# One condition for the middle and the long arm of an expert block, a branch hint for the next block in both, and 49 narrow idle products at the head in place of 15 wide ones

## The chip, the cores and the metric

The kernel runs on one core of one Trainium2 chip. The metric is device microseconds (us) of one execution, median of several. TensorE (PE) multiplies, with its weight loads shown as an engine of their own (PEld); VectorE (DVE), ScalarE (ACT) and GpSimd (POOL) do the rest; SyncE (SP) issues most transfers.

## The reference

```python
attn_out = sigmoid(q k^T / sqrt(64) - log(448)) v       # 4 x 12 heads, 448 tokens
x = attn_out as 1792 tokens x 768
do_compute = x @ w_skip > 0                              # other tokens pass as they are
e_idx = argmax(xc @ w_gate); gate_w = softmax prob. of that expert
for e in range(8):                                       # 768 -> 1024 -> 768
    y[mask] = gate_w * (relu(xc[mask] @ w1[e]) @ w2[e])
x[do_compute] = xc + y
h = x @ w_in; g = elu(h); out = g @ w_out                # 768 -> 2048 -> 768
```

Everything is float32. The kernel gets that accuracy out of products on split operands: a high and a low part of each side, three products per tile.

## The kernel before

The work runs in three stages: attention (up to about 200 us of the span), the experts (about 200 to 420 us), and the last dense layer pair (to the end). The order on PE, ACT and DVE is written out by hand; only semaphores between engines hold an instruction back.

At the very head `keep_warm` lets PE multiply zeros while the first q and k come in: 15 products, each 512 columns wide, each with its own weight load.

The routing sorts the tokens that compute into blocks of 256 slots, each block for one expert, full blocks first. Block 0 is done ahead of the routing's end (`first_block`). For the others the code is unrolled in `level(i, k)`, i = 1 to 14, each nested in the one before; how many of them run, and which way, is known only on the chip. `k` is the kind of block i, read from `kinds`: 0 no block, 1 at most 128 rows, 2 up to 64 rows in the second half, 3 more than that. With these inputs blocks 1 and 2 are of kind 3, blocks 3 and 4 of kind 2, blocks 5 to 7 of kind 1, and block 8 doesn't exist (the token counts of each expert give it, and the four places of `rest`'s product, in the table below, agree).

In program order, the code of one level is:

- condition `more{i}` (k > 0); else the way out (`close(i)`, far behind, after all levels)
- `between(i)`: 12 flips of the block's rows into columns, and chunks 5 and 6 of the block before (24 products)
- condition `two{i}` (k > 1); else the **short arm**
- `lead_in(i)`: chunk 7 of the block before (12 products)
- condition `few{i}` (k == 2): the **middle arm**, `expert(i, k, (P, FEW))`; else `rest()`
- condition `many{i}` (k == 3): the **long arm**, `expert(i, k, (P, P))`; else `rest()`
- the short arm: `lead_in(i)` and `expert(i, k, (P,), following)`
- then level i + 1

`rest()` is one tiny product, one tiny ACT copy and one tiny DVE copy into a tile of its own. `skips(label, value)` gives PE's sequencer a hint for the condition of that label: 1, it will fall through; 0, it will jump. The hints of before: `two{i}` at the start of a level, `few{i}` ahead of `lead_in`, `many{i}` inside the middle arm, `more{i+1}` inside the short arm.

The weights come in 8 chunks per expert of 128 x 1536, each split by ACT (L547, high part) and DVE (L549, low part) two chunks ahead of PE.

Of the kernel before, what the change touches and what calls it, by code (L numbers as in the profile page):

```python
# [12 lines left out]
F32 = mybir.dt.float32  # L13
# [10 lines left out]
P = 128  # L24
# [14 lines left out]
NB = 1 + (NT + E * (BLK - 1)) // BLK  # L39
# [12 lines left out]
FEW = 64  # L52
# [39 lines left out]
def build(nc, tc, a):  # L92
    q, k, v, consts = a["q"], a["k"], a["v"], a["consts"]
    wg, w1, w2, wi, wo, out = a["wg"], a["w1"], a["w2"], a["wi"], a["wo"], a["out"]
    wide = [w[f].bitcast(I32) for f in range(KF2) for w in (wi, wo)]
    with ExitStack() as top:
# [6 lines left out]
        cst = cp.tile([P, LASTING], F32, name="cst")  # L103
# [10 lines left out]
        iota_h = cp.tile([P, P], F16, name="iota_h")  # L114
# [62 lines left out]
        with ExitStack() as st:  # L177
# [16 lines left out]
            pss = pst.enter_context(tc.tile_pool(name="pss", bufs=3, space=PSUM))  # L194
# [7 lines left out]
            zero_b = xp.tile([P, 1, P], BF16, name="zero_b")  # L202
            nc.gpsimd.memset(zero_b, 0.0)

            def keep_warm(n):

                ps = pss.tile([P, 4, P], F32, name="idle", tag="ps")
                for _ in range(n):
                    nc.tensor.matmul(
                        ps, zero_b[:, 0], zero_b.to_broadcast([P, 4, P]), start=True, stop=True  # L210
                    )

            keep_warm(15)
            xT = xp.tile([P, NP, NT], F32, name="xT")
            lgT = xp.tile([P, RING * P], F32, name="lgT")

# [488 lines left out]
            def tiles(pool, names, shape, dt=F32):  # L705
                return [pool.tile([P, *shape], dt, name=n) for n in names]
# [3 lines left out]
            acc_t = tiles(psb, [f"acc{j}" for j in range(6)], [512])  # L710
# [31 lines left out]
            def routing():  # L742
# [58 lines left out]
                for k_, p in enumerate(counted):  # L801
                    nc.tensor.matmul(
                        ordered, ones_b, p, start=(k_ == 0), stop=(k_ == len(counted) - 1)
# [34 lines left out]
                for t in range(NTT):  # L838
# [17 lines left out]
                tokb = st.enter_context(  # L856
                    tc.tile_pool(name="tokb", reuse_waits="tile", bufs=1, side="right")
                )
                for e in range(2):
                    rest_t.append(iter(tiles(tokb, [f"rest{e}{j}" for j in range(2 * NB)], [1])))  # L860
                hs_t.extend(tiles(tokb, ["hs0", "hs1"], [N1]))
                hf_t.extend(tiles(tokb, ["hf0", "hf1"], [N1]))
                yf_t.extend(hf[:, :N2] for hf in hf_t)
# [9 lines left out]
                yield  # L873
                order_rows()

            rest_t, hs_t, hf_t, yf_t, one_hot = [], [], [], [], []
            last_rows, last_gate, last_slot = [], [], []

            def h_columns(nh, sizes):
# [41 lines left out]
            def ahead(i, c, **parts):  # L921
                c += 2
                split_w(i + c // 8, c % 8, **parts)
# [21 lines left out]
            def up_two(i, soon):  # L945
                for c in range(4):
                    ahead(i, c)
                    for f in range(4):
                        if (c, f) == (0, 1):
                            soon()  # L950
                        up_one(i, c, f)
                        if c % 2:
                            h_one(4 * (c // 2) + f)

            def up_parts(i, sizes, soon):
                for h, n in enumerate(sizes):
                    if n < P:
                        t = h * P
                        nc.scalar.copy(x2[:, 0, :, t + n : t + P], x2[:, 1, :, t : t + n])
                ahead(i, 0)  # L960
                for nh in range(2):
                    for c3 in range(2):
                        c = 2 * nh + c3
                        for h, n in enumerate(sizes):
                            o = acc_t[nh if n == P else (3, 0)[nh]]
                            product(o, h, n, x_part, i, c, N1, 3 * c3, KD)
                        if c == 0:
                            soon()
                        ahead(i, c + 1)
                        if nh == 1 and c3 == 0:  # L970
                            h_columns(0, sizes)
                    for n in sizes:
                        if n == P:
                            nc.scalar.copy(hs_t[nh], acc_t[nh])
                        else:
                            nc.scalar.copy(hf_t[nh], acc_t[(3, 0)[nh]])

            def back(i, h, n, chunks):

                for c in chunks:  # L980
                    c4, nh = divmod(c - 4, 2)
                    product(py[nh][h], h, n, h_part, i, c, N2, 4 * c4, KF1)
                    if n < P and c4:
                        nc.scalar.copy(yf_t[nh], py[nh][h])
# [23 lines left out]
                slot_order()  # L1008
                return kind(1)

            def expert(i, k, sizes, following=None):
                whole = sizes == (P, P)

                def soon():
                    outcome(i - 1, 0, P)

                if whole:
                    up_two(i, soon)
                    ahead(i, 4)
                else:  # L1020
                    up_parts(i, sizes, soon)
                    if len(sizes) > 1:
                        skips(f"many{i}", 1 - (k >> 1))
                    elif i + 1 < NB:
                        skips(f"more{i + 1}", (following + 3) >> 2)
                ahead(i, 5)
                for h, n in list(enumerate(sizes))[1:]:
                    if whole:
                        back(i, h, n, range(4, 8))
                        outcome(i, h, n)  # L1030
                        back(i, 0, P, range(4, 5))
                    else:
                        back(i, h, n, range(4, 6))
                        h_columns(1, sizes)
                        back(i, h, n, range(6, 8))
                        back(i, 0, P, range(4, 5))
                        outcome(i, h, n)
                if len(sizes) == 1:
                    back(i, 0, P, range(4, 5))
                    h_columns(1, sizes)  # L1040

            def outcome(i, h, n):
                gated(xg_t[i % NXG][h], slot_gate[:, 2 * i + h : 2 * i + h + 1], h, n)
# [32 lines left out]
            def pass_on(i):  # L1076

                gather(i + 1)
                if i > 1:
                    scatter(i - 2)
# [86 lines left out]
            def close(i):  # L1172
                if i == 1:
                    gather(1)
                s = 2 * (i - 1)
                nc.gpsimd.tensor_copy(last_rows[0], xg_t[(i - 1) % NXG][0])
                nc.gpsimd.tensor_copy(last_gate[0], slot_gate[:, s : s + 1])
                nc.gpsimd.tensor_copy(last_slot[0], slot_tok[:, s : s + 1])
                give(xg_t[(i - 1) % NXG][1], slot_tok[:, s + 1 : s + 2])
                for g in range(3):  # L1180
                    flip_rows(i, g, ends[g])
                for g in range(3):
                    flip_rows(i + 1, g, later[g])
# [21 lines left out]
            def kind(i):  # L1205
                return nc.values_load(kinds[:1, i : i + 1], min_val=0, max_val=3)

            def skips(label, unless=0):

                tc.mark_branch_hint_location(label, hint=unless, engines=[ET.PE])  # L1210

            def rest():

                nc.tensor.matmul(acc_t[5][:, :2], iota_h, iota_h[:, :2], start=True, stop=True)
                nc.scalar.copy(next(rest_t[0]), cst[:, :1])
                nc.vector.tensor_copy(next(rest_t[1]), cst[:, :1])

            def level(i, k):
                pass_on(i)
                if i == NB:  # L1220
                    close(i)
                    return
                with tc.If(k > 0, label=f"more{i}") as more:
                    skips(f"two{i}", k >> 1)
                    fetch(i, range(2, 8))
                    between(i)
                    fetch(i + 1, range(2))
                    following = kind(i + 1) if i + 1 < NB else 0
                    with tc.If(k > 1, label=f"two{i}") as both:
                        skips(f"few{i}", 1 - (k & 1))  # L1230
                        lead_in(i)
                        with tc.If(k == 2, label=f"few{i}") as arm:
                            expert(i, k, (P, FEW))
                        with arm.Else():
                            rest()
                        with tc.If(k == 3, label=f"many{i}") as arm:
                            expert(i, k, (P, P))
                        with arm.Else():
                            rest()
                    with both.Else():  # L1240
                        lead_in(i)
                        expert(i, k, (P,), following)
                    level(i + 1, following)
                with more.Else():
                    close(i)
# [229 lines left out]
```

## Time and profile before

| | |
|---|---|
| median of 3 runs | 904.13 us (903.27 to 906.42) |
| the profiled execution | 903.78 us, of which the span from first to last instruction is 902.0 us |
| PE, its busy share | 880.9 us, 98% |
| PEld | 710.4 us, 79% |
| DVE, ACT, POOL | 62%, 54%, 9% |
| `rest`'s product (L1214) | 4 times: at 214.1, 249.3, 310.2 and 346.5 us |

A row of the timeline reads: start, duration, engine, line, operation, output <- inputs, shapes, count, and in brackets how long the engine sat idle before it and what ended that; "issue" there means that it waited for nothing that the profile shows. "q8 instruction" among the DMA queues is code on its way to an engine.

### The profile page before, as it was taken

The page shows a single profiled execution, that of the slowest core. Times are in us where ns is not written, and L with a number is a line of the kernel's source. Part 1 is how long each engine was busy: PE and PEld are TensorE (multiplying, and loading weights), DVE is VectorE, ACT ScalarE, POOL GpSimd, SP SyncE. Part 2 cuts the span into 40 slices and gives each one's busy share as a digit, 9 for nine tenths or more (in the row PEclk, how much of TensorE's full clock was granted, in tenths as well). Part 3 has the DMA queues.
Part 4 walks back from the last instruction along what each step waited for, and adds up shares of the span by engine and source line. Part 5 has one row for each costly group of instructions (what it writes and reads, how often), then busy time and mean ns, then how long its engine had stood idle before and what let it go on. Part 6 is the DMA issues. An engine that isn't in the chain of part 4 may idle for free.

```text
span 902.0 us, 13626 instructions
## 1 busy us (share of the span) xinstructions
PE 880.9 (98%) x5208; PEld 710.4 (79%) x5208; DVE 557.5 (62%) x872; ACT 485.5 (54%) x680; POOL 80.8 (9%) x79
## 2 busy tenths in 40 slices
PE   9999999999999898998999999999999999999998
PEld 4445545699999787887888888888888888888997
DVE  2968778697666465885888886444344444344664
ACT  7777776554455464773645554434444434344664
POOL 1000000112101022332100000100000100000100
PEclk9999999999999999999999999999999999999999
DMA  8788875779956175955733430100000100000100
GB/s 291 260 281 274 302 262 200 262 276 405 373 181 232 45 293 202 410 215 197 242 96 102 123 105 19 70 1 18 18 18 19 70 1 1 1 1 18 53 1 36
DMA packets 34194, 134.71 MB, mean 149 GB/s; under 512 B 4698, under 2 KB 5850, under 8 KB 34098
## 3 DMA queue, kind: packets, MB, share of 16 engines
q1 hardware_dynamic: 29474, 114.22, 35.6%
q0 software_dynamic: 4480, 19.01, 5.9%
q8 instruction: 56, 0.92, 0.4%
q14 instruction: 40, 0.33, 0.1%
q10 hardware_dynamic: 144, 0.23, 0.1%
HBM read 112.47 MB, written 23.99 MB: 151 GB/s over the span
## 4 chain that ended last, share of the span: by engine, by line
PE 54%; issue 0%; DVE 0%; ACT 0%; ACTq 0%
PE acc L1350 16%; PE pt L1350 10%; PE acc L1318 9%; PE acc L1319 9%; PE acc L1317 8%; PE acc L142 1%; PE acc L1201 0%; PE acc L556 0%; PE acc L557 0%; PE acc L558 0%; DVE both L573 0%; ACT both L571 0%; ACT raw L1361 0%; ACTq L1471 0%; ACTq L571 0%
## 5 line engine op out<-in xcount | busy, mean ns | idle before, releaser
L549 DVE TENSOR_TENSOR wlo<-raw,whi 128x1536 fp32r<-128x1536 f32 x64 | 111.7, 1763 | 28.4 <-ACT whi L547 27.0
L1328 DVE SCALAR_TENSOR_TENSOR m<-m,acc 128x512 f32<-128x512 f32 (+1 forms) x64 | 39.7, 620 | 139.4 <-ACT m L1327 139.4
L1326 ACT ACTIVATE m<-acc 128x512 f32<-128x512 f32 (+1 forms) x64 | 34.9, 545 | 167.9 <-PE acc L1319 158.4
L547 ACT CAST whi<-raw 128x1536 fp32r<-128x1536 f32 x64 | 93.9, 1483 | 17.3 <-PE acc L558 6.6
L249 ACT ACTIVATE at<-ps,bias 112x896 f32<-112x896 f32 x96 | 88.9, 1010 | 23.3 <-PE ps L242 23.0
L1350 PE MATMUL acc<-wol,gh 128*128 128x256 f32 x320 | 100.8, 315 | 0.0
L1350 PE MATMUL acc<-woh,gl 128*128 128x256 f32 x320 | 100.4, 314 | 0.0
L1350 PE MATMUL acc<-woh,gh 128*128 128x256 f32 x320 | 100.4, 314 | 0.0
L1318 PE MATMUL acc<-x,wih 128*128 128x512 f32 (+1 forms) x270 | 96.2, 356 | 0.0
L1317 PE MATMUL acc<-x,wih 128*128 128x512 f32 (+1 forms) x270 | 96.2, 356 | 0.0
L1319 PE MATMUL acc<-x,wil 128*128 128x512 f32 (+1 forms) x270 | 96.1, 356 | 0.0
L556 PE MATMUL acc<-whi,both 128*128 128x384 f32 (+1 forms) x236 | 83.9, 355 | 2.7 <-DVE both L573 1.6
L557 PE MATMUL acc<-wlo,both 128*128 128x384 f32 (+1 forms) x236 | 82.9, 351 | 0.6 <-DVE wlo L549 0.6
L558 PE MATMUL acc<-whi,both 128*128 128x384 f32 (+1 forms) x236 | 82.5, 350 | 0.0
L256 PE MATMUL po<-at,vt 112*64 112x448 f32 x384 | 77.5, 545 | 0.0
L1306 DVE TENSOR_TENSOR wol<-wo,woh 128x768 fp32r<-128x768 f32 x64 | 61.2, 956 | 23.4 <-ACT woh L1305 23.0
L1350 PEld LDWEIGHTS acc<-woh,gh 128*128 128x128 f32 x320 | 60.3, 188 | 9.9
L1350 PEld LDWEIGHTS acc<-wol,gh 128*128 128x128 f32 x320 | 60.3, 188 | 9.5
L1305 ACT CAST woh<-wo 128x768 fp32r<-128x768 f32 x64 | 53.3, 833 | 26.0 <-PE acc L1350 25.9
L1332 DVE TENSOR_TENSOR gl<-m,gh 128x512 fp32r<-128x512 f32 (+1 forms) x64 | 40.0, 626 | 40.5 <-ACT gh L1331 40.5
L1350 PEld LDWEIGHTS acc<-woh,gl 128*128 128x128 f32 x320 | 60.1, 188 | 4.2
L1300 DVE TENSOR_TENSOR wil<-wi,wih 128x768 fp32r<-128x768 f32 x60 | 57.4, 956 | 7.6 <-ACT wih L1299 6.9
(268 smaller groups left out, 1872.2 us busy)
## 6 DMA issues: line engine op xcount, KB each, us to landing
raw<-in_w SPq DMA_DIRECT2D x66, 768.0 KB, 12.4
raw<-in_wi SPq DMA_DIRECT2D x9, 768.0 KB
raw<-in_wo SPq DMA_DIRECT2D x9, 768.0 KB, 7.1
vt<-in_v SPq DMA_DIRECT2D x12, 448.0 KB, 6.4
raw<-in_wi SPq DMA_DIRECT2D x14, 384.0 KB
raw<-in_wo SPq DMA_DIRECT2D x14, 384.0 KB, 3.1
qr<-in_q SPq DMA_DIRECT2D x11, 448.0 KB, 4.3
kr<-in_k SPq DMA_DIRECT2D x11, 448.0 KB, 4.1
```

Of the source, the lines that this page charges most:

```text
L249: nc.scalar.activation(at[:, :, c, :], ps[:CP, :, :S], AF.Sigmoid, bias=bias[:CP], scale=QK_SCALE)
L256: nc.tensor.matmul(po[64 * j : 64 * j + 64, :S], vt[:, 2 * (hp % 2) + j, c, :], at[:, j, c, :], start=(c == 0), stop=(c == NCH - 1),)
L547: nc.scalar.copy(w_hi, raw)
L549: nc.vector.tensor_sub(w_lo, raw, w_hi)
L556: nc.tensor.matmul(o, a_hi, b_hi, start=first, stop=False)
L557: nc.tensor.matmul(o, a_hi, b_lo, start=False, stop=False)
L558: nc.tensor.matmul(o, a_lo, b_hi, start=False, stop=last)
L1306: nc.vector.tensor_sub(pair[1], wo_r[f], pair[0])
L1317: nc.tensor.matmul(o, a, b, start=(cc == 0), stop=False)
L1318: nc.tensor.matmul(o, a, c, start=False, stop=False)
L1319: nc.tensor.matmul(o, wil[:, cc], b, start=False, stop=(cc == KD - 1))
L1350: nc.tensor.matmul(o, a, b, start=(clears and f == 0 and k_ == 0), stop=(f == KF2 - 1 and k_ == 2), skip_group_check=True,)
```

## The change

`keep_warm` runs 49 products of 160 columns (5 x 32), each with its own load, in place of 15 of 512. In `level` the two conditions `few{i}` and `many{i}` become one: middle arm if k == 2, else the long arm. `rest()` and its tiles are gone. The hint `many{i}` is gone; the middle and the long arm now give the hint for `more{i+1}` that only the short arm gave. Tiles, arithmetic and the order of work inside an arm stay.

```diff
             def keep_warm(n):
-                ps = pss.tile([P, 4, P], F32, name="idle", tag="ps")
+                ps = pss.tile([P, 5, 32], F32, name="idle", tag="ps")
+                idle = zero_b[:, :, :32].to_broadcast([P, 5, 32])
                 for _ in range(n):
-                    nc.tensor.matmul(
-                        ps, zero_b[:, 0], zero_b.to_broadcast([P, 4, P]), start=True, stop=True
-                    )
-
-            keep_warm(15)
+                    nc.tensor.matmul(ps, zero_b[:, 0], idle, start=True, stop=True)
+
+            keep_warm(49)
...
-                for e in range(2):
-                    rest_t.append(iter(tiles(tokb, [f"rest{e}{j}" for j in range(2 * NB)], [1])))
...
-            def expert(i, k, sizes, following=None):
+            def expert(i, sizes, following):
...
                     up_parts(i, sizes, soon)
-                    if len(sizes) > 1:
-                        skips(f"many{i}", 1 - (k >> 1))
-                    elif i + 1 < NB:
-                        skips(f"more{i + 1}", (following + 3) >> 2)
+                if i + 1 < NB:
+                    skips(f"more{i + 1}", (following + 3) >> 2)
...
-            def rest():
-
-                nc.tensor.matmul(acc_t[5][:, :2], iota_h, iota_h[:, :2], start=True, stop=True)
-                nc.scalar.copy(next(rest_t[0]), cst[:, :1])
-                nc.vector.tensor_copy(next(rest_t[1]), cst[:, :1])
-
...
                         with tc.If(k == 2, label=f"few{i}") as arm:
-                            expert(i, k, (P, FEW))
+                            expert(i, (P, FEW), following)
                         with arm.Else():
-                            rest()
-                        with tc.If(k == 3, label=f"many{i}") as arm:
-                            expert(i, k, (P, P))
-                        with arm.Else():
-                            rest()
+                            expert(i, (P, P), following)
                     with both.Else():
                         lead_in(i)
-                        expert(i, k, (P,), following)
+                        expert(i, (P,), following)
```

## Rows read from the trace of the kernel before

**Rows 1.** The page, part 1: busy us (share of the span) and instructions

```profile
PE 880.9 (98%) x5208; PEld 710.4 (79%) x5208; DVE 557.5 (62%) x872; ACT 485.5 (54%) x680; POOL 80.8 (9%) x79
```

**Rows 2.** Waits of PE: line waited for, us in total, times, longest

```profile
PE pt L142 <- issue: 2.0, 1, 2.0
...
PE acc L556 <- issue: 1.5, 2, 1.2
...
PE pt L142 <- DVE rest L1216: 1.0, 1, 1.0
```

**Rows 3.** Timeline, end of block 3 (middle arm) and start of block 4

```profile
308.92 1.45 PE L1051 MATMUL acc<-hf,cst 128*128 128x384 f32 x4
309.77 1.26 DVE L1052 SCALAR_TENSOR_TENSOR xg<-acc,slot_gate,xg 128x384 f32<-128x384 f32 x2 [5.86 <-PE acc L1051]
...
310.21 0.17 PE L1214 MATMUL acc<-iota_h 128*128 128x2 f16 x1
310.95 0.14 DVE L1216 COPY rest<-cst 128x1 f32<-128x1 f32 x1
...
312.43 1.06 PE L142 MATMUL pt<-cst,xg 128*128 128x128 f32 x8 [2.05 <-issue]
```

**Rows 4.** Timeline, end of block 4 (middle arm) and start of block 5

```profile
346.48 0.17 PE L1214 MATMUL acc<-iota_h 128*128 128x2 f16 x1
347.42 0.15 DVE L1216 COPY rest<-cst 128x1 f32<-128x1 f32 x1
...
347.63 1.09 PE L142 MATMUL pt<-cst,xg 128*128 128x128 f32 x8 [0.98 <-DVE rest L1216]
```

**Rows 5.** Timeline of PE, the condition two5 (block 5 takes the short arm)

```profile
352.98 0.34 PE L558 MATMUL acc<-whi,both 128*128 128x384 f32 x1
354.50 0.45 PE L556 MATMUL acc<-whi,both 128*128 128x384 f32 x1 [1.18 <-issue]
```

**Rows 6.** DMA by queue, 420 to 880 us: packets, MB, share of 16 engines

```profile
q8 instruction: 19, 0.31, 0.3%
```

**Rows 7.** Busy time by stretch: us, PE busy (x) PEld busy (x) DVE, ACT, POOL

```profile
420.00:880.00 460.00, 459.96 (x2447) 393.22 (x2447) 254.92 (x415) 217.40 (x358) 21.15 (x21) 1.00 0.16 53
214.10:249.30 35.20, 34.84 (x254) 34.46 (x253) 21.34 (x24) 15.81 (x20) 5.77 (x6) 1.00 0.95 370
320.00:346.65 26.65, 25.71 (x134) 20.97 (x133) 13.87 (x13) 12.54 (x16) 4.40 (x3) 1.00 0.46 182
354.45:367.95 13.50, 13.45 (x69) 11.88 (x70) 11.13 (x10) 9.37 (x9) 5.72 (x4) 1.00 1.02 411
```

**Rows 8.** DMA by queue, 305.0 to 305.2 us

```profile
q8 instruction: 1, 0.02, 29.6%
```

**Rows 9.** DMA by queue, 309.3 to 309.5 us

```profile
q8 instruction: 1, 0.02, 35.8%
```

**Rows 10.** DMA by queue, 345.2 to 345.4 us

```profile
q8 instruction: 1, 0.02, 44.6%
```

**Rows 11.** DMA by queue, 352.0 to 352.2 us

```profile
q8 instruction: 1, 0.02, 30.0%
```

**Rows 12.** DMA by queue, 354.0 to 370.2 us

```profile
q8 instruction: 1, 0.02, 0.4%
```

**Rows 13.** Timeline of PEld at the head

```profile
1.03 0.13 PEld L209 LDWEIGHTS <-zero_b 128*128 128x128 bf16 x2 [1.03 <-POOL zero_b L203]
...
4.42 0.15 PEld L209 LDWEIGHTS <-zero_b 128*128 128x128 bf16 x1 [0.28 <-issue]
4.85 0.97 PEld L209 LDWEIGHTS <-zero_b 128*128 128x128 bf16 x5 [0.28 <-issue]
6.24 0.17 PEld L242 LDWEIGHTS ps<-qh,kh 64*112 64x112 f32 x2 [0.42 <-issue]
```

**Rows 14.** Timeline of ACT at the head

```profile
6.62 0.57 ACT L234 CAST kh<-kr 128x448 fp32r<-128x448 f32 x1 [0.92 <-DMA kr<-in_k]
7.15 1.01 ACT L249 ACTIVATE at<-ps,bias 112x896 f32<-112x896 f32 x1
```

More of the change, by code (lines that the diff above doesn't have):

```diff
@@ L874, in routing @@
                 order_rows()
-            rest_t, hs_t, hf_t, yf_t, one_hot = [], [], [], [], []
+            hs_t, hf_t, yf_t, one_hot = [], [], [], []
             last_rows, last_gate, last_slot = [], [], []
```

## The prediction

> **What bounds the kernel now.** Read the page's busy times first: PE is busy for 98% of the span [rows 1], so only what stops PE, or adds products to it, moves the end. The waits of PE come next, as the change touches the experts' branches: of those that end at a block's edge, 2.0 us are "issue" at L142, up to 1.2 us "issue" at L556, and 1.0 us is the wait for `rest`'s DVE copy [rows 2]. "Issue" means that PE waited for nothing shown. The timeline tells where. Block 3 ends with `rest` at 310.21, the DVE copy at 310.95 + 0.14 = 311.09, and PE starts block 4 at 312.43: 1.3 us beyond what DVE explains [rows 3]. Block 4 ends alike, but PE starts block 5 at 347.63, right behind the DVE copy (347.57) [rows 4]. And at condition two5 the next product, due 0.17 after 352.98, starts at 354.50: 1.2 to 1.3 us lost [rows 5].
>
> The DMA view explains these three. The queue "q8 instruction" is PE's code: from 420 to 880 us it has 19 packets [rows 6] while PE ran 2447 products and 2447 loads [rows 7], so one 16 KB packet holds about 4894/19 = 258, that is 256, instructions. Packets come at 305.0 and 309.3 ahead of the late start at 312.43 [rows 8, 9], and at 352.0 ahead of the late one at 354.50 [rows 11]. So PE's sequencer, which runs ahead of PE, stops at a jump into code that is not there yet. A packet's booking to PE's restart takes 3.1 us (309.3 to 312.43) or 2.4 us (352.1 to 354.50); two in a row come 4.3 us apart (305.0, 309.3).
>
> **The jump that loses its hint.** Count instructions (two per product) from the code and [rows 7]: the long arm has 204 products (254 in its stretch, less `rest`, the 48 of the next lead-in and a straddler), 408 instructions; the short arm 68 (69 with a straddler), 136. So from the middle arm's end over the long arm (landing) and over the short arm to level i + 1 it is 408 + 136 + some 6 = 550: more than two packets. Before, the hint `many{i}` in the middle arm brought in the landing's packet early, and only the last short hop could miss. After, the arm's end is an unconditional jump without a hint, and the new hint `more{i+1}` has the value 1 at blocks 1 to 6: it promises falling through and asks for nothing.
>
> Whether that costs depends on where packets end. An estimate from rows: from 354.0 to 370.2 one packet comes [rows 12], the one in order behind the short arm's. From the short arm's start to the next block's condition are 138 + 77 = 215 instructions; had they crossed into the next packet, a second would have been called. So block 5's short arm starts s = 0 to 41 instructions behind an edge, and block 5 itself, 791 = 3 x 256 + 23 ahead of it, at s - 23. After the change 34 more products put 68 instructions ahead of everything, and each level is some 7 shorter (both `rest`s, one condition, two fewer for the hint): block 5 starts at s - 23 + 68 - 28 = s + 17, its landing 139 earlier, at s - 122, one packet before, and the middle arm's end at s - 533, for s below 21 two packets before the landing. So at block 4 to 5 both hops miss. The same count for block 3 to 4 puts the landing in the packet next in order, which is there: one late packet, as before.
>
> **The sum.** (a) Block 4 to 5: the packet at 345.2 [rows 10] is what that jump calls now; after, it would be the landing's, the next 4.3 later at 349.5, and PE restarts 2.4 to 3.1 behind it, at 351.9 to 352.6, not 347.63 [rows 4]: +4.3 to +5.0, I take +4.6. Below: +0.4, if one packet suffices (345.2 + 2.4 to 3.1 = 347.6 to 348.3). (b) two5: its hint now lies with the condition in one packet, so its target can be called from 351 on and be there when block 5's 36 products of 0.17 us are done near 358; the 1.26 us [rows 5] would go, but the call stands behind the packet in order. Between -1.26 and +3 (a call 4.3 late, as in the pair above); nearest to the row that shows a call out of a fresh packet, so half the gain, -0.6. (c) Block 3 to 4: -1.3 (DVE is the next bound, 311.1) to 0; without `rest` the jump is called a little sooner, -0.3. (d) `rest`: four products of 0.17 us and the DVE copy's 0.15 at 347.42 lie before a late packet now; 0, at most -0.4. ACT's wait for it at the long arm delays splits that PE doesn't wait for: 0. (e) Two hint instructions in the long arm: 0 beside 204 products. [...]
>
> 903.78 + 4.6 - 0.6 - 0.3 = 907.5 us, against the profiled execution, 0.35 below the median of the runs shown.
>
> **Rivals.** *The jump costs nothing or one packet* (same): the sequencer runs far enough ahead, or block 5 lies with its landing in one packet. For it: only one of two such jumps was late before, and the edge is an estimate. Against: the hint did the covering. Then 903.78 + 0.4 - 0.3, or -0.6 more: 903.3 to 904.2. [...]
>
> *All late packets go* (faster): no stop at block 4 to 5, (c) at -1.3, (b) at -1.26, (d) at -0.4: 900.8. It needs every edge to fall well; it decides from the landing and the next start lying in packets already in.
>
> *One more late target* (slower still): two6 stays in one packet with its hint now; 33 more instructions put the condition at s + 215 + 33 = s + 248, over an edge for s of 8 and more. Its target is then called when the sequencer reaches the edge, late in the block; at two5 this cost 1.26, here with less cover up to 3.4: 907.5 + 3.4 = 910.9.
>
> **How the numbers follow.** Both hops miss, 907.5: 0.36, own range 905.5 to 909. With two6 late, 911: 0.22. Same, 903.7: 0.35. Faster, 900.8: 0.07. This kernel can tell about 0.3%, 2.7 us, from no change: below 901.4 or above 906.8. Of the first case a seventh may stay under 906.8, hence slower 0.53, same 0.40, faster 0.07. The range runs from 902.5 (below it only the faster case) to 912.5 (two6 and the upper end of (b) together lie above).
>
> **What would show it.** Right: PE idle of some 5 us, "issue", between L1051's end and L142 at block 4 to 5, two q8 packets some 4 us apart ahead of it; two5 with less than its 1.18 idle; block 3 to 4 within 0.5 us of before; the first scores within 1 us of 6.24. Wrong: block 5 starting within 0.5 us of DVE's last L1052 there; or a stop in blocks 1 and 2, which jump over the middle arm with the same hint as before; or scores that begin past 7.5, with PE still at the wide spacing.

## The result and the profile after

The changed kernel takes 916.75 us (median of 4, 913.80 to 919.89), the kernel before, run beside it, 903.94 us (903.27 to 906.42): a ratio of 1.0134, 95% interval 1.0102 to 1.0166. It is slower, by 12.8 us, where 907.5 (902.5 to 912.5) was forecast. The profiled execution took 915.26 us, its span is 913.5: 11.5 us more than before's 902.0.

The page of the changed kernel, part 1 (busy us, share of the span, instructions), to lay beside [rows 1]:

```profile
PE 885.9 (97%) x5238; PEld 718.8 (79%) x5238; DVE 557.2 (61%) x868; ACT 485.2 (53%) x676; POOL 76.8 (8%) x79
```

PE is busy 5.0 us longer, although the work is the same (but for 34 more idle products at the head, and without `rest`'s four), and idle 6.5 us longer. Its waits (line waited for: us in total, times, longest), beside [rows 2]:

```profile
PE pt L142 <- issue: 8.7, 2, 4.6
PE pt L142 <- DVE both L892: 4.5, 3, 1.5
PE acc L555 <- issue: 3.7, 2, 3.1
```

L142 is still the flips at a block's start; L555 is what L556 was. "Issue" has gone from 3.5 to 12.4 us, in four places. (A number behind a condition is its level: few1 is `few{i}` of block 1.) The timeline of PE at the jump of condition few1 into block 1's long arm, and at the starts of blocks 4 and 5, which answer to [rows 3, 4]:

```profile
212.29 0.34 PE L557 MATMUL acc<-whi,both 128*128 128x384 f32 x1
215.75 0.58 PE L555 MATMUL acc<-both,whi 128*128 128x256 f32 x1 [3.13 <-issue]
216.13 0.42 PE L556 MATMUL acc<-both,whi 128*128 128x256 f32 x1
...
312.30 1.45 PE L1046 MATMUL acc<-hf,cst 128*128 128x384 f32 x4
...
317.85 1.88 PE L142 MATMUL pt<-cst,xg 128*128 128x128 f32 x8 [4.10 <-issue]
...
352.25 1.45 PE L1046 MATMUL acc<-hf,cst 128*128 128x384 f32 x4
...
358.33 1.42 PE L142 MATMUL pt<-cst,xg 128*128 128x128 f32 x8 [4.63 <-issue]
...
366.16 0.45 PE L555 MATMUL acc<-whi,both 128*128 128x384 f32 x1 [0.56 <-issue]
```

The first stop is new: before, block 1's long arm began without one. The second was 2.05 [rows 3], the third 0.98 [rows 4], the last, at two5, 1.18 [rows 5]. Behind the first stop a 256-column product takes 0.42 us (before: 0.28), behind the second eight flips take 1.88 (before: 1.06). The table by stretch says why (PE's busy time and count come first; PEclk, the third number from the end, is the granted clock as a share of full speed). The last row is of the kernel before, behind its stop of 2.05 us:

```profile
215.70:219.20 3.50, 3.45 (x17) 3.45 (x18) 1.06 (x1) 0.00 (x0) 0.00 (x0) 0.54 1.02 392
219.20:230.00 10.80, 10.80 (x94) 10.80 (x93) 3.95 (x6) 4.27 (x6) 0.00 (x0) 1.00 0.91 371
317.80:321.30 3.50, 3.45 (x15) 3.48 (x16) 1.45 (x3) 1.85 (x4) 0.00 (x0) 0.52 0.11 40
...
358.30:362.40 4.10, 4.07 (x19) 4.10 (x20) 2.07 (x3) 2.93 (x4) 0.00 (x0) 0.58 0.07 23
...
312.40:316.00 3.60, 3.57 (x25) 3.60 (x26) 1.88 (x3) 2.86 (x4) 0.00 (x0) 1.00 0.89 279
```

After each of the three stops the granted clock is 0.52 to 0.58 over the next 3.5 to 4.1 us; behind the first it is 1.00 again from 219.2 on (the second row). In the kernel before, the same work was granted 1.00 after a stop of 2.05 us.

PE's sequencer has rows of its own, which tell how long a jump stood (line, operation, count: ns min/median/max, first and last start in us). Here are the changed kernel's at few1 and at the ends of blocks 3 and 4, and then the kernel before's at the end of block 3, where two hops follow each other:

```profile
L1221 PEldq COMPARE_BRANCH  x1: 6333/6333/6333, 209.4 to 209.4; - x1
...
L1221 PEldq COMPARE_BRANCH  x1: 6350/6350/6350, 311.0 to 311.0; - x1
...
L1221 PEldq COMPARE_BRANCH  x1: 6866/6866/6866, 351.0 to 351.0; - x1
...
L1236 PEldq COMPARE_BRANCH  x2: 444/1836/3229, 308.2 to 308.7; - x2
```

The jump out of the middle arm is reached at 311.0 and 351.0, 1.3 us before the fold products (L1046) begin, and each of the three stands for 6.3 to 6.9 us; the one late hop of before stood 3.2. The code packets of the waits at blocks 3 and 4, one in each, are booked only at 314.9 and 355.4, 3.9 and 4.5 us after the jump was reached and 2.9 ahead of PE's restart; before, it was 0.6 after the jump (308.7 to 309.3). The queue in 314.8 to 315.0 and in 355.3 to 355.5 us:

```profile
q8 instruction: 1, 0.02, 31.9%
...
q8 instruction: 1, 0.02, 31.8%
```

Taking the same product in both traces gives the lag of the changed kernel, step by step. It starts at -1.65 us where the experts begin (196 us in before): the wait of 1.1 us for gathered rows at the end of attention is not there this time, and the first scores start 0.36 earlier.

| step | us | lag behind it |
|---|---|---|
| few1: the stop | +3.16 | 1.51 |
| slower clock behind it, less a stop of 0.4 that before had there | +0.94 | 2.45 |
| products of blocks 1 and 2, a little slower each | +0.93 | 3.38 |
| block 3 to 4: the longer stop | +2.04 | 5.42 |
| slower clock behind it | +1.64 | 7.06 |
| block 4 to 5: the longer stop | +3.64 | 10.70 |
| slower clock behind it | +1.59 | 12.29 |
| two5: the shorter stop | -0.63 | 11.66 |
| the rest, to the end of block 7 | -0.17 | 11.49 |

So three late jumps cost 8.8 us of idle time and 4.2 us by the slower clock behind them.

### The profile page after: what moved, and what is told of

The parts are those of the page before. It is cut to its first block, busy times and chain, and to the rows that moved or that the text cites. A ratio compares the mean times of both kernels' runs of the same rounds, so it can differ in the third digit from the quotient of the medians.

```text
span 913.5 us, 13640 instructions
## 1 busy us (share of the span) xinstructions
PE 885.9 (97%) x5238; PEld 718.8 (79%) x5238; DVE 557.2 (61%) x868; ACT 485.2 (53%) x676; POOL 76.8 (8%) x79
## 4 chain that ended last, share of the span: by engine, by line
PE 53%; issue 0%; ACT 0%; ACTq 0%
PE acc L1335 16%; PE pt L1335 10%; PE acc L1303 8%; PE acc L1304 8%; PE acc L1302 8%; PE acc L142 1%; PE acc L1196 0%; PE acc L555 0%; PE acc L557 0%; PE acc L556 0%; ACT both L570 0%; ACT raw L1346 0%; ACTq L1456 0%; ACTq L570 0%; ACTq L1212 0%
## 5 line engine op out<-in xcount | busy, mean ns | idle before, releaser
L555 PE MATMUL acc<-whi,both 128*128 128x384 f32 (+1 forms) x236 | 84.6, 358 | 2.1 <-ACT both L570 1.5
L556 PE MATMUL acc<-wlo,both 128*128 128x384 f32 (+1 forms) x236 | 83.5, 354 | 0.6 <-DVE wlo L548 0.6
```

The costliest lines, as they stand in the source:

```text
L555: nc.tensor.matmul(o, a_hi, b_hi, start=first, stop=False)
L556: nc.tensor.matmul(o, a_hi, b_lo, start=False, stop=False)
```

## The experiments

Fourteen kernels ran. All but those said to be edits of the changed kernel are edits of the kernel before. "A stop" is PE idle by "issue" ahead of the named place. Ratios are to the kernel before, with 95% intervals.

**The head alone.** The first half of the change, with the old branches.

```diff
-            keep_warm(15)
+            keep_warm(49)
```

(and the 5 x 32 columns of the change.)

> The kernel before with the new head (49 products of 160 columns) and its old branches. All code behind the head stands 68 instructions later, as in the changed kernel. Theory A (late code after jumps costs the time, and where a packet of 256 ends decides whether a hint comes early enough): the 3.1 us stop ahead of block 1's long arm appears here too, since its hint and condition fall on the same places, with up to 1.3 us of slower clock behind it; the ends of blocks 3 and 4 keep the hint for the landing, so their stops stay at 0 to 2 us; first scores 0.36 us earlier. Together 904 to 909 us. Rival B (the merged branches alone cost it, whatever the alignment): no stop at block 1, 903.5 us. Rival C (the shift alone explains all of the loss): stops of 4 us at the ends of blocks 3 and 4 as well, 912 us or more.

918.28 us, 1.0158 (1.0134 to 1.0182): the head alone costs more than the whole change. Waits of PE:

```profile
PE acc L555 <- issue: 4.5, 2, 3.5
...
PE acc L557 <- issue: 3.5, 1, 3.5
PE acc L1213 <- issue: 3.4, 1, 3.4
PE pt L142 <- DVE rest L1215: 2.5, 2, 1.7
```

The stop ahead of block 1's long arm (L1213 is `rest`'s product there) is there as theory A had it, and the end of block 3 waits for `rest`'s DVE copy alone, 0.77. The 1.74 at the end of block 4 is put down to that copy too, but the copy ends at 350.73 and PE starts at 351.55: a hop stands there for 3.05 us, its packet booked at 348.6. What A didn't have are 3.45 at two5, 1.07 at two6 and 3.48 inside block 6's short arm. So A's time failed, and C's came out, but not at C's places.

**The branches alone.** The changed kernel with 15 products of 512 columns.

> The changed branches with the old head (15 products of 512 columns), so the code of block 1 stands where it stood before. Theory A: no stop ahead of block 1's long arm; the ends of blocks 3 and 4 jump without a hint over 550 instructions to code that is not there: stops of 4.1 to 4.7 us (before: 2.05 and 0.98) and some 1.6 us of slower clock behind each, so 903.9 + 2.1 + 1.6 + 3.7 + 1.6 = 912.9 us, one us either way for two5 to two7. Rival C (the shift by the head explains the loss): stops at the ends of blocks 3 and 4 as before, 904 us. Rival E (with these positions one late packet suffices at one of the two): 908 us.

912.60 us, 1.0095 (1.0069 to 1.0121), where A had 912.9. No stop ahead of block 1's long arm, 3.93 and 5.07 at the ends of blocks 3 and 4:

```profile
PE pt L142 <- issue: 9.0, 2, 5.1
PE pt L142 <- DVE both L893: 4.5, 3, 1.5
PE acc L556 <- issue: 2.2, 3, 1.1
```

Each half costs by itself, and they don't add: 14.6 and 8.9 us alone, 12.8 together. The merged code is 6 to 7 instructions shorter per level, so blocks 5 to 7 stand elsewhere, and the stops of the head alone at two5 and two6 are not there.

**The new hints taken out** of the middle and the long arm of the changed kernel.

```diff
-                if i + 1 < NB:
+                if len(sizes) == 1 and i + 1 < NB:
                     skips(f"more{i + 1}", (following + 3) >> 2)
```

> The changed kernel without the new hints for the next block in the middle and the long arm (the short arm keeps its own). Theory A: these hints promise falling through and call nothing, so the stops ahead of block 1's long arm (3.1 us), at the end of block 3 (4.1) and of block 4 (4.6) stay within 0.5 us each; 913 to 918 us, as the changed kernel. Rival F (the new hints displace the packet that is needed): these stops shrink to what they were before or less; 903 to 908 us.

920.30 us, 1.0171 (1.0141 to 1.0202). The stops are 3.11 at block 1, 3.99 at the end of block 3, and 7.67 at the end of block 4, where A had 4.6. F falls: the hints displace nothing. The 7.67 are two packets in a row, booked at 356.4 and 359.6, with PE's restart at 362.46: block 5 stands 16 instructions earlier in this kernel, and the places counted below would put a packet's end right at its start.

**The arms swapped** in the changed kernel.

```diff
-                        skips(f"few{i}", 1 - (k & 1))
+                        skips(f"few{i}", k & 1)
...
-                        with tc.If(k == 2, label=f"few{i}") as arm:
-                            expert(i, (P, FEW), following)
+                        with tc.If(k == 3, label=f"few{i}") as arm:
+                            expert(i, (P, P), following)
                         with arm.Else():
-                            expert(i, (P, P), following)
+                            expert(i, (P, FEW), following)
```

> The changed kernel with the two arms in the other order: long arm if k == 3, else the middle arm, the hint's value turned to match. The middle arm now ends in front of the short arm, so its end jumps over 138 instructions instead of 550; the long arm's end jumps over 268 + 138 = 406 instead of 138. Theory A: the stops at the ends of blocks 3 and 4 shrink to 0 to 2 us, and new ones of 3.5 to 4.7 us, with slower clock behind them, come at the ends of blocks 1 and 2 (in the changed kernel: none); the stop ahead of block 1's long arm goes, as block 1 falls through there, and conditions few3 and few4 now jump over 411 with a hint and may stop up to 3 us each; 909 to 918 us. Rival G (the missing rest and its pause cost the time, not the distance): stops of 4 us stay at the ends of blocks 3 and 4, and none comes at the ends of blocks 1 and 2.

908.55 us, 1.0069 (1.0044 to 1.0095). The ends of blocks 3 and 4 have no stop left, with no `rest` in the kernel, so G falls. The jump that is now long shows it instead, at the end of block 1 only:

```profile
PE pt L142 <- issue: 3.2, 1, 3.2
PE acc L555 <- issue: 3.2, 4, 1.1
```

At the end of block 2, by the count some 922 instructions further on, the same jump stops nothing; 0.86 us are lost 21 products behind it, in straight code. A had a stop at both. That fits a jump of 406 which leads past the packet next in order from one place and into it from another, but no run shows that directly.

**The shift without the narrow products.** 49 products at the head, 43 of them 2 columns wide.

```diff
-                for _ in range(n):
+                for j in range(n):
...
+                    if j < n - 6:
+                        nc.tensor.matmul(ps[:, 0, :2], zero_b[:, 0], zero_b[:, 0, :2], start=True, stop=True)
+                    else:
+                        nc.tensor.matmul(ps, zero_b[:, 0], wide, start=True, stop=True)
...
-            keep_warm(15)
+            keep_warm(49)
```

> The kernel before, its branches untouched, with a head of 49 products too, but 43 of them only 2 columns wide and 6 of 512: the code behind it stands 68 instructions later, as in the head alone, without its 160-column products. Theory A (only the place of the code against the packets of 256 matters): the stops of the head alone come back within 0.5 us each: 3.4 ahead of block 1's long arm, 3.5 at two5, 1.1 and 3.5 behind two6; 915 to 920 us, with up to 2 us at the head either way. Rival H (the 160-column products do it, through the clock or the order of work in attention): no such stops, 903 to 906 us.

917.11 us, 1.0142 (1.0118 to 1.0166). The stops of the head alone are back one by one, though the two heads share only their count of products. Waits of PE, and then its timeline inside block 6's short arm:

```profile
PE acc L558 <- issue: 4.2, 2, 3.1
PE acc L560 <- issue: 3.6, 1, 3.6
PE acc L1216 <- issue: 3.5, 1, 3.5
```

```profile
385.07 0.34 PE L559 MATMUL acc<-wlo,both 128*128 128x384 f32 x1
388.99 0.48 PE L560 MATMUL acc<-whi,both 128*128 128x384 f32 x1 [3.58 <-issue]
```

The last stop stands in straight code, eleven products behind two6's target, in both kernels: no jump, no wait, only the next packet, which in this run is booked at 386.2, 2.8 us ahead of PE's restart. H falls; the place of the code is the cause.

**The hint for few given earlier** in the changed kernel, ahead of `between`.

```diff
                     skips(f"two{i}", k >> 1)
+                    skips(f"few{i}", 1 - (k & 1))
...
-                        skips(f"few{i}", 1 - (k & 1))
                         lead_in(i)
```

> The changed kernel with the hint for few given at the start of the level, beside the one for two, some 76 instructions earlier. Theory A1 (at block 1 the hint fires too late): the 3.1 us stop ahead of block 1's long arm shrinks to 0 to 1 us and the slower clock behind it goes: 4 us faster than the changed kernel, 911 to 914 us. Theory A2 (a target is only called once the packet with the condition itself has come up): the stop stays at 3.1 us; 915 to 918 us. The stops at the ends of blocks 3 and 4 stay above 3.9 us in both.

914.87 us, 1.0136 (1.0102 to 1.0169). The program of this kernel holds no hint for few at all: given there, it falls out. So it answers another question: without the hint the stop at block 1 is 1.36, with it 3.13 (the jump itself stands 4.57 for 6.33). The gain is lost at the end of block 4, where block 5 stands 16 instructions earlier, as in the run without the new hints, and two packets in a row (352.8, 356.0) make a stop of 8.46.

**Another shift, 40 instructions,** with 35 products of 224 columns, under the old and the changed branches.

```diff
-            keep_warm(15)
+            keep_warm(35)
```

> The kernel before with 35 idle products of 224 columns: 7840 columns as in the changed head, but the code stands 40 instructions later, not 68. Counted from the places where products stopped in the runs so far, no hint stands across a packet's end from its condition at block 1, two5, two6 and two7. Theory A: the stop ahead of block 1's long arm is below 0.5 us, the one at the end of block 3 below 1 us, two6 has none; two5 is open (0 to 3.5 us, as it came at 3.5 with 68 and at 1.2 with 0): 902 to 908 us. Rival H (narrow idle products at the head cost it): 915 us or more.

> The changed kernel with 35 idle products of 224 columns in place of 49 of 160: its code stands 28 instructions earlier. Theory A: no stop ahead of block 1's long arm (hint and condition in one packet), which saves 3.1 us and 1 us of slower clock; the ends of blocks 3 and 4 jump without a hint as before and stop for 3.9 to 5.1 us each, with slower clock behind them; 910 to 914 us. Rival (only the alignment costs it): 905 us or less.

917.96 us, 1.0140 (1.0117 to 1.0163), and 919.35 us, 1.0150 (1.0129 to 1.0170). Theory A failed as it stood: with hint and condition in one packet by the count, the stop ahead of block 1's long arm is 3.22 and 3.07, two5 3.60 and two6 3.30 (old branches). So either a hint that stands ahead of its condition in the same packet is not enough, or the count of places is off. H's time came out, but the run with 2-column products has these stops without any narrow product of H's kind; the rival of the second run fell. In the changed form PE starts block 5 after 5.28 us, does one flip, and stops again:

```profile
360.39 0.45 PE L142 MATMUL pt<-cst,xg 128*128 128x128 f32 x1 [5.28 <-issue]
363.45 0.80 PE L142 MATMUL pt<-cst,xg 128*128 128x128 f32 x3 [2.62 <-issue]
```

**A whole packet, and two small shifts,** by 2-column products at the head as above: 143 products (138 narrow), 22 (8) and 25 (11).

> The kernel before, its branches untouched, with a head of 143 products: 138 of 2 columns, then 5 of 512. The code behind it stands 256 instructions later, one whole packet. Theory A (the place within packets of 256 decides): every stop comes back as in the kernel before: none above 0.5 us at block 1, 2.0 at the end of block 3, 1.0 at the end of block 4, 1.2 at two5, none at two6; 903.7 us, with up to 1.5 us more from the longer head. Rival (more instructions ahead of the experts are simply worse, or another packet size): stops of 3 us and more, 910 to 918 us.

> The kernel before with 22 idle products, 8 of 2 columns and 14 of 512: its code stands 14 instructions later. Theory A: at the end of block 3 the condition stands 14 instructions further behind a packet's edge, so its target is called earlier and the stop falls from 2.05 to DVE's bound of 0.8; at two5 the edge is crossed 14 instructions sooner, so its 1.2 us falls to 0.3; the rest as before: 903.7 - 1.3 - 0.9 = 901.5 us, faster than both kernels. Rival (a shift this small moves nothing, or moves some other target over an edge): 903.7, or 906 and more with a new stop of 3 us.

> As the shift by 14, but with 25 idle products, 11 of 2 columns and 14 of 512: 20 instructions later. Theory A: the same gains, 901.5 us, if block 5 still begins ahead of the edge (it is counted to stand at most one or two instructions ahead of it); if it has come to stand behind it, the end of block 4 needs one more packet: a stop of 1.5 to 4 us there in place of 1.0, 904 to 907 us. Rival: as before, 903.7 us.

905.94 us, 1.0025 (1.0013 to 1.0037); 905.44, 1.0011 (1.0000 to 1.0023); 904.72, 1.0013 (1.0002 to 1.0024). With 256 instructions more, the 13 to 15 us of 40 and 68 instructions are gone, and the stops are those of before: 0.50 in block 1, 1.85 and 0.98 at the ends of blocks 3 and 4; only two5's is missing. So the place counts within a packet of 256. The small shifts gained nothing: at 14, the stop at the end of block 3 stayed at 2.04, and two5's grew to 1.50; at 20 they are 1.75 and 0.87, but the stop inside block 1's long arm (below) takes 1.74. Neither is faster than the kernel before.

They also show a packet's end directly. In block 1's long arm PE stops once in straight code; the first product behind the stop, for shifts of 14 and 20:

```profile
217.31 0.39 PE L560 MATMUL acc<-both,wlo 128*128 128x256 f32 x1 [1.16 <-issue]
```

```profile
215.96 0.38 PE L560 MATMUL acc<-both,wlo 128*128 128x256 f32 x1 [1.74 <-issue]
```

Counted from the arm's first product in the timeline, the stop comes after 21 products in the kernel before, 14 with a shift of 14, 11 with 20, and 21 again with 256. Two instructions per product (5208 products and 5208 loads in [rows 1]) make that one fixed place, or one a whole packet on. The nearer the arm's start it lies, the longer the stop: 0.36, 1.16, 1.74.

**The hint for many turned to 1,** every instruction at its place.

```diff
-                        skips(f"many{i}", 1 - (k >> 1))
+                        skips(f"many{i}", 1 - (k >> 2))
```

> The kernel before with one value turned: the hint for many in the middle arm always says falling through (1), so nothing is called ahead for the jump over the long arm. Both conditions, rest, the head and every instruction's place stay as they are. Theory A (what the merge costs is the lost call ahead): the stops at the ends of blocks 3 and 4 grow to 4 to 5 us each or more (before: 2.05 and 0.98), with slower clock behind them, and no stop comes at block 1: 911 to 915 us, as the merged branches alone (912.6). If both hops then miss one after the other, 7 to 8 us at one of them, 915 to 919 us. Rival I (the hint called nothing in time anyway; the merge costs by its missing pause or its own layout): 904 us.

910.15 us, 1.0058 (1.0040 to 1.0076). A half hit. At block 4 the hint does what the prediction said it does: without its call the landing's packet is booked at 345.9, the next at 349.1, two5's target only at 356.6, and PE stops at each step:

```profile
348.44 0.18 PE L1214 MATMUL acc<-iota_h 128*128 128x2 f16 x1 [1.03 <-issue]
...
349.19 1.06 PE L142 MATMUL pt<-cst,xg 128*128 128x128 f32 x8 [0.57 <-issue]
...
351.69 0.44 PE L557 MATMUL acc<-wlo,both 128*128 128x384 f32 x1 [0.82 <-issue]
...
359.08 0.55 PE L556 MATMUL acc<-whi,both 128*128 128x384 f32 x1 [3.13 <-issue]
```

But at block 3 the stop stays at 2.07: there the hint's value changes nothing, and neither end comes to the 4 to 5 us of the merged form.

**`rest` taken out,** both conditions and their hints kept.

```diff
                             expert(i, k, (P, FEW))
-                        with arm.Else():
-                            rest()
...
                             expert(i, k, (P, P))
-                        with arm.Else():
-                            rest()
```

> The kernel before with its two conditions and its hints, but without rest: where an arm is skipped, nothing runs but the semaphore's own instruction. The code of block 5 stands 12 instructions earlier, that of block 1 unmoved. Theory A (the hop to the landing and its hint are what calls the next packets early; rest only takes time): the stops at the ends of blocks 3 and 4 stay at or below 2.0 and 1.0 us, two5 within 1.5 us: 902.5 to 905.5 us. Rival G (without rest's pause the jump runs into code that is not there): stops of 4 us and more at the ends of blocks 3 and 4, 910 us or more.

911.58 us, 1.0078 (1.0065 to 1.0092): A's time is missed, its places hold. The ends of blocks 3 and 4 stop for 2.23 and 0.94, so `rest` is not what the merged form lacks. The loss is again a place: block 5 stands 12 instructions earlier, and its short arm now stops in straight code, with 2.5 us of slower clock behind it (384-column products start 0.32 us apart, 0.17 ahead of the stop), and another 1.9 us come at the way out behind block 7:

```profile
360.97 0.48 PE L558 MATMUL acc<-whi,both 128*128 128x384 f32 x1 [3.96 <-issue]
```

**The hint for few turned to 1** in the changed kernel, every instruction at its place.

```diff
-                        skips(f"few{i}", 1 - (k & 1))
+                        skips(f"few{i}", 1 - (k >> 2))
```

> The changed kernel with one value turned: the hint for few always says falling through (1), every instruction at its place. Theory A3 (at block 1 a hint that calls the long arm delays the packet in order, which holds that arm anyway; told by the run in which that hint fell out): the stop ahead of block 1's long arm falls from 3.1 to about 1.4 us and the slower clock behind it goes; the ends of blocks 3 and 4 stay at 4.1 and 4.6: 912 to 915 us. Rival J (the stop fell there because the code of the level was shorter): 3.1 us as in the changed kernel, 914 to 918 us.

918.32 us, 1.0160 (1.0146 to 1.0175). The stop ahead of block 1's long arm falls from 3.13 to 1.79 in the profiled execution. It is put down to ACT's whi there, but the jump itself still stands, 4.99 us for 6.33, and PE starts 0.06 behind it. So it is the hint's value and not the code's length that lengthens this stop, and J falls there. The other half of A3 failed: the slower clock stays behind the shorter stop (0.65 over 4.9 us):

```profile
214.80:219.70 4.90, 4.90 (x28) 4.90 (x29) 2.37 (x3) 0.00 (x0) 0.56 (x1) 0.65 1.02 377
```

The time doesn't follow: the two profiled executions have spans of 913.4 and 913.5 us. The 1.3 us gained at few1 are given back: the clock behind the ends of blocks 3 and 4 (stops of 4.59 and 3.80, then 1.94 us for eight flips both times) costs 0.5 us more each than in the changed kernel, and the experts start 0.4 us later.

## Why the prediction was wrong

**The direction and the half that was worked out.** Slower was the likeliest case, and step (a) named the right jump. The term (a), +4.6, measured +3.64 of idle time and +1.59 of slower clock: 5.2. Its "both hops miss" was wrong in form. The middle arm's jump now goes to the next level at once, and one packet is booked for it, not two. But this one jump stands 6.87 us, twice as long as a late hop of before, with its packet booked at 355.4 and PE's restart 2.9 behind that. That the size came near is luck: no run shows what fills the first 4.5 us.

Step (b), -0.6 at two5, measured -0.63, and that is luck too. The target isn't called earlier: two5's jump stands 3.36 us, for 3.03 before (first the kernel before, then the changed one):

```profile
L1229 PEldq COMPARE_BRANCH  x1: 3028/3028/3028, 351.4 to 351.4; - x1
...
L1218 PEldq COMPARE_BRANCH  x1: 3357/3357/3357, 362.7 to 362.7; - x1
```

The slower clock behind block 4's end kept PE busy for 1.59 us longer with the products ahead of two5, and so less of the wait was left to show as idle time. Steps (d) and (e) cost nothing that shows. At the head the wide spacing of the idle loads [rows 13] is not there: 49 of them run from 1.02 to 5.75, and the first scores start at 5.88, for 6.24 before. But ACT's second kh, which waits for k to land, starts 0.30 earlier as well, at 6.32 [rows 14], and in the head alone, with the same 49 products, the scores start at 7.23; so the lead can't be put down to the head.

**The step that failed first: the 68 instructions were counted into two jumps only.** The prediction used the shift to place block 5 and its landing, and for the rest took the places of before as they were: "a stop in blocks 1 and 2, which jump over the middle arm with the same hint as before" stood among what would prove it wrong. That stop came, +3.16 and about 1 us of clock: few1's jump, which had stood 0.40 us before, stood 6.33. The head alone (918.28) and the same shift without its columns (917.11) show that the places are worth more than the branches: with the old branches this shift costs 13 to 15 us, and a shift by a whole packet 1.7. It was in reach: the prediction itself counted in packets of 256.

**The second: (c), block 3 to 4 "as before".** It was given -0.3 and measured +2.04 and +1.64 of clock. The count was right, one late packet; the time of its booking was not. Before, it was booked at 309.3, 0.4 us after the folds began [rows 3, 9]; after, at 314.9, 2.6 us after them. The jump is not reached later than before: the way out of the arm is reached at 307.9 and 311.0, both times some 2.5 us before PE runs out of work (310.4 and 313.8). The merged jump only stands longer, 6.35 us. With both conditions and the old head this stop is 2.05, 2.07 and 2.23, whatever the hint said and with or without `rest`. And it is the merge, not a place, that does it: in the nine kernels with both conditions, under shifts of 0 to 256 instructions, no stop at the ends of blocks 3 and 4 is longer than 2.23; in the six with merged branches in this order every one is 3.8 to 8.5, and the jump there stands 6.0 to 8.1 us. What the nine share, and the merged form lacks, is the landing between the arms. That the landing is what helps was only argued: no run put one into the merged form.

**The third: the price of a stop.** The prediction ended a stop where PE restarts. Behind the six stops of 3 us and more in the experts of the changed kernel and of the head alone, the granted clock was 0.50 to 0.62 over the next 2.8 to 4.4 us. In the changed kernel that cost 1.5 to 1.6 us more each (few1: 1.5, less the stop that before had there), 4.2 us of 11.5.

With the three put right from the trace, the sum is: (a) 5.23, few1 and its clock 4.10, (c) 3.68, (b) -0.63, the products' pace 0.93, the gather's wait and the head -1.65, the remainder -0.17: 11.49 us.

The measurement decides against the rival in which the jump costs nothing: a jump of 550 forward stops PE for 3.8 us and more in six kernels, and one of 406 for 3.2 at one of its two places. The run shifted by 256 agrees with packets of 256 instructions, as the prediction counted them (905.94 us, with the stops of before but for two5's). And the packets at 314.9 and 355.4 are booked behind the jumps that stood, in line with a jump that waits for its code.

**What stays open.** Why a jump over 406 instructions was late at block 1 and not at block 2 fits the packet's place, but the exact rule by which the sequencer calls ahead was not found: the count by hints and conditions failed for the shift of 40 instructions. Nor is it known why some late jumps stand 3 to 4 us and others about 6 and more. Distance alone doesn't decide: two5's jump, over the same arms, stood 3.03 before and 5.94 in the head alone. In the branches alone, at the end of block 3, a packet is booked just after the jump is reached (309.2) and another 3.4 us later; in the changed kernel nothing is seen on the queue in that time. So the time at a new shift can't be forecast yet from the code alone. It is open, too, why the 256-column products of blocks 1 and 2 took 281 ns each in the changed kernel and 276 before, at a granted clock of 1.00 in both.

## What to carry to other kernels

Where a kernel's code branches and TensorE is the bound, every instruction added or removed ahead moves all jumps behind it against the packets, of 256 instructions here (68 more cost 13 to 15 us, 256 more 1.7): repeat a measurement under a few shifts (2-column products at the head took 0.03 us each) before an edit is judged by its time. Count for every jump that the data takes, hinted or not, how far it leads and where packets end, look up in the trace how long it stood, and be wary of merging two hops into one long jump, which cost 3.7 and 5.2 us here. Price a stop with the slower clock behind it: 1.5 to 1.6 us more here, behind each of the stops of 3.1 to 4.6 us in the changed kernel.

## What the runs showed that was not expected

- 40 or 68 instructions more ahead of the experts cost 13 to 15 us (1.4 to 1.6%); 14, 20 or 256 cost 0.5 to 2 us.
- A hint can lengthen a stop: 3.13 us with the hint for few at block 1, 1.36 and 1.79 without it or with its value turned (one profiled execution each).
- A stop in straight code, 3.5 to 4.0 us long, eight to eleven products behind a jump that had itself been waited for.
- 43 products of 2 columns took 1.31 us at the head, 0.03 each.
- Behind the stops of 3 us and more in the experts of the changed kernel and of the head alone the granted clock was 0.50 to 0.62 over the next 2.8 to 4.4 us. Behind stops of about 2 us it was low in one place (0.65 over 4.9 us, behind 1.79 with the hint for few turned) and 1.00 in another (behind 2.05 in the kernel before); behind 2.19 (the 2-column shift, block 4) and 2.23 us (`rest` taken out, block 3) eight flips took 1.06 as ever.
